# First loads on two queues, gate values behind them, own places for the last batch's second part, and a reordered last group, in an attention and two-layer MoE kernel on one core

## The chip, the cores and the metric

The kernel runs on one core of a Trainium2 chip. The metric is the device time of one execution in microseconds (us), here as the median of several runs. Five engines work side by side: TensorE (PE in the profile, PEld for its weight loads), VectorE (DVE), ScalarE (ACT), GpSimd (POOL) and SyncE (SP). DMA transfers are put in a queue by an engine: rows marked SPq are the instructions of SyncE's queue.

## The reference

The reference is attention with a gated memory, followed by two feed-forward networks over the same 2304 tokens, all in float32:

```
local = softmax(causal(q @ k^T / 8)) @ v                # B=4, H=8, S=576, D=64
qp    = elu(q) + 1
mem   = (qp @ M_prev) / (qp . z_prev + 1e-6)
g     = 1 / (1 + exp(-beta))                            # one gate per head
x     = g * mem + (1 - g) * local                       # 2304 x 512
x     = elu(x @ w_in) @ w_out                           # 512 -> 2048 -> 512
out   = leaky_relu(x @ w2_in, 0.01) @ w2_out            # 512 -> 2048 -> 512
```

The weights come in as float64 and are brought to float32 on the chip.

## The kernel before, in words

**Order of the work.** The function `tile_attn_moe_kernel` traces instructions in an order that is also their priority. A scheduler of the language, which runs when the kernel is built, then puts each engine's instructions into a fixed order by simulated times. On the chip every engine works through its own list in that order, and so does SP with its queue: an instruction that waits holds up all behind it on its engine. `keep_in_program_order(ins)` pins an instruction behind what was traced last on its engine; `issue_after(ins)` puts what a block traces on the engine of `ins` behind `ins` in that engine's list.

**Start.** Before anything else the gate values are made (lines 83 to 87): `beta` is loaded on SP's queue, ScalarE takes the exponential (`ging`), VectorE adds one, takes the reciprocal (`gat`) and makes `omg`. Only `norm` (line 451, `omg`) and `phi_unit` (line 393, `ging`) read them, both later. Attention runs over 4 batches with 4 pairs of heads each. `Pair.load_qk` (lines 265 to 269) loads a pair's keys and then its queries with `load_rows` (line 209), four transfers each, all on SP's queue; `load_rest` loads values, `z_prev` and `M_prev`. TensorE turns keys (`k_unit`, line 294) and queries (`q_unit`, line 312), ScalarE and VectorE copy them out of PSUM, and `score` (line 426) follows.

**Weights.** `load_w` (line 93) fetches a slice f of 128 columns of one network (16 slices) into `wraw` and decodes it. Behind attention that is a chain on one buffer `wm`: ScalarE line 127, VectorE lines 128, 129 and 132, ScalarE cast (`copy`, line 241), GpSimd line 138 twice; then line 127 of the next slice. Slices 0 to 6 of the first network lie in the pool `wpa` and are decoded during attention. Slices 7 to 15 lie in `wpb`, in places w0 to w8, where attention's tiles were before.

**First network, narrow part.** `phase1_units(ti)` (line 663) works on batch ti in two parts of 288 tokens, with slices 0 to 6. `u_load` (line 667) fetches a part: for batches 1 to 3 the attention result lies in two arrays in DRAM (`xq_scr`), so four transfers bring tile `x` and its mirror `y`. `u_x` (line 678) adds `y` to `x` (line 682, four instructions on VectorE), casts to `xh` on ScalarE (line 610) and takes the rest `xl` on GpSimd (line 614). `u_h` (matmuls of line 621, elu of lines 631 to 636 with the cast `gh` at line 243 and `gl` at line 628) and `u_o` (matmuls of line 649) follow. There is one tile `x` and one tile `y` for both parts; the second part's load is traced after slice 1 of the first part, its `u_x` before slice 4 in the last batch, elsewhere before slice 6.

**Last batch.** What is left of the units after attention is the list `side` (line 781). The loop of lines 796 and 797 traces units until `u_x` of the last batch's first part has noted its last cast as `pools["cast", 0]`; the first two decodes of slices 7 and 8 are traced under `issue_after` of that cast (line 800).

**First network, wide part.** Lines 849 to 893 run over five groups of tokens (512 each, the last 256) with slices 7 to 15: line 621 with `xw` and `xv`, elu, line 649 into four PSUM banks. The next group's `h` matmuls use other input tiles and can go before. **Second network.** Lines 899 to 932: per group 16 slices of line 621, `leaky`, and `emit_o3` (matmuls of line 911), one slice after the other with all token blocks (`tb`) of 128 in each. At the end of a group each bank goes out in two halves through a tile `st` with two buffers: VectorE copy (line 931), store on SP's queue (line 932). The last group has two blocks.

Of the kernel before, what the change touches and what calls it, by code (L numbers as in the profile page):

```python
# [8 lines left out]
F32 = mybir.dt.float32  # L9
# [6 lines left out]
P = 128  # L16
# [3 lines left out]
def _f(ap):  # L20
    return ap.bitcast(F32)
# [3 lines left out]
def kernel(  # L25
# [54 lines left out]
    gat = const.tile([P, H], F32, name="gat")  # L80
    ging = const.tile([P, H], F32, name="ging")
    omg = const.tile([P, H], F32, name="omg")
    nc.sync.dma_start(bet, beta.partition_broadcast(P))
    nc.scalar.activation(out=ging, in_=bet, func=AF.Exp, scale=-1.0)
    nc.vector.tensor_scalar(out=ging, in0=ging, scalar1=1.0, scalar2=None, op0=ALU.add)
    nc.vector.reciprocal(gat, ging)
    nc.vector.tensor_scalar(out=omg, in0=gat, scalar1=-1.0, scalar2=1.0, op0=ALU.mult, op1=ALU.add)


    wi_tiles = {}  # L90
    wo_tiles = {}
# [114 lines left out]
    def bank(tag):  # L206
        return psum.tile([P, 512], F32, tag=tag, bufs=BANKS[tag], name=tag)

    def load_rows(dst, src, b, hp, dup):

        hs = slice(2 * hp, 2 * hp + 2)
        for ca, cb, r0 in ((0, 2 if dup else 3, 0), (3, 5, 320)):
            for j in range(2):
                nc.sync.dma_start(
                    dst[:, ca:cb, j * D:(j + 1) * D],
                    src[b, 2 * hp + j, r0:r0 + (cb - ca) * P, :].rearrange("(c p) d -> p c d", p=P),
                )
        for r in range(2 if dup else 0):
            nc.sync.dma_start(
                dst[64 * r:64 * r + 64, 2, :].rearrange("p (j d) -> p j d", j=2),  # L220
                src[b, hs, 256:320, :].rearrange("j p d -> p j d"),
            )
# [29 lines left out]
    class Pair:  # L252
# [12 lines left out]
        def load_qk(self):  # L265
            self.q = at.tile([P, 5, P], F32, tag="qn", bufs=1, name="qn")
            self.k = at.tile([P, 5, P], F32, tag="kn", bufs=1, name="kn")
            load_rows(self.k, k, self.b, self.hp, False)
            load_rows(self.q, q, self.b, self.hp, False)

        def load_rest(self):
            b, hp = self.b, self.hp
# [277 lines left out]
    def attention_units():  # L550

        pairs = [Pair(ti, hp) for ti in range(len(tiles1)) for hp in range(NHP)]
        keys = [(pr, j, g) for pr in pairs for j in range(2) for g in pr.groups]
        items = [Item(*key, n) for n, key in enumerate(keys)]
        first = {}
        for n, it in enumerate(items):
            first.setdefault(id(it.pr), n)
        units = [(0, pairs[0].load_qk, None), (0, pairs[0].load_rest, None)]
        def prep(pi):
            pr = pairs[pi]  # L560
            l = [(PC, lambda g=g: pr.k_unit(g)) for g in pr.kgroups]
            l += [(PC, lambda g=g: pr.q_unit(g)) for g in pr.groups]
            l += [(0, pr.phi_unit)]
            if pi + 1 < len(pairs):
                l.append((0, pairs[pi + 1].load_qk))
            return l

        units += [(c, u, None) for c, u in prep(0)]
        for n in range(len(items) + 2):
            lists = []  # L570
            if n < len(items):
                it = items[n]
                pr = it.pr
                pi = pairs.index(pr)
                head = []
                if first[id(pr)] == n:
                    head.append((0, pr.v_unit))
                    if pi + 1 < len(pairs):
                        head.append((0, pairs[pi + 1].load_rest))
                if n + 1 < len(items) and items[n + 1].pr is not pr:  # L580
                    lists.append(("prep", prep(pi + 1)))
                lists.append(("score", head + it.stages()[0]))
            if 1 <= n <= len(items):
                lists.append(("tr", items[n - 1].stages()[1]))
            if n >= 2:
                it = items[n - 2]
                c = list(it.stages()[2])
                if first[id(it.pr)] == n - 2:
                    c = [(PC, lambda g=g, pr=it.pr: pr.qp_unit(g)) for g in it.pr.groups] + c
                lists.append(("pv", c))  # L590
            w = weave(*lists)
            done = None
            if n >= 2 and (n == len(items) + 1 or items[n - 1].pr.ti != items[n - 2].pr.ti):
                done = items[n - 2].pr.ti
            units += [(c, u, None) for c, u in w[:-1]] + [(w[-1][0], w[-1][1], done)]
        return units
# [4 lines left out]
    def mtile(tag, bufs, dt=F32, shape=None):  # L601
        shape = shape or (NW,)
        pool = pools.get(("own", tag), pools["mlp"])
        return pool.tile([P] + list(shape), dt, tag=tag, bufs=bufs, name=tag)
# [58 lines left out]
    def phase1_units(ti):  # L663

        mine = [(pi, o, w, {}) for pi, (pt, o, w, _) in enumerate(parts) if pt == ti]

        def u_load(pi, o, w, st):
            xt = st["t"] = mtile("x", 1, F32, (NKC, NW))[:, :, 0:w]
            if ti < V32:
                nc.sync.dma_start(xt, xm_scr[ti][:, :, o:o + w])  # L670
                return
            x2 = st["t2"] = mtile("y", 1, F32, (NKC, NW))[:, :, 0:w]
            for j in range(2):
                ps, pz = slice(64 * j, 64 * j + 64), slice(64 - 64 * j, 128 - 64 * j)
                nc.sync.dma_start(xt[ps], xq_scr[ti][j][ps, :, o:o + w])
                nc.sync.dma_start(x2[ps], xq_scr[ti][j][pz, :, o:o + w])

        def u_x(pi, o, w, st):
            xt = st["t"]
            if ti >= V32:  # L680
                for c in range(NKC):
                    add = nc.vector.tensor_tensor(out=xt[:, c], in0=xt[:, c], in1=st["t2"][:, c], op=ALU.add)
                    if c == 0 or ti < len(tiles1) - 1:
                        tc.keep_in_program_order(add)
            st["x"] = split_x(xt, w, pi % 2)
            for n in range(2):
                nc.sync.dma_start(xp_scr[n][pi], _f(st["x"][n]))
            st["g"] = {}

        units = [(0, lambda: u_x(*mine[0]))]  # L690
        for k, (pi, o, w, st) in enumerate(mine):

            def u_h(f, w=w, st=st):
                ph = h_bank()[:, 0:w]
                h_mm(ph, wi_tiles[0, f], *st["x"])
                st["g"][f] = elu(ph, w)

            def u_o(ec, pi=pi, w=w, st=st):
                py = bank("sc" if tail else "pm")[:, 0:w]
                o_mm(py, range(NFA), 0, ec, st["g"], 0, NFA - 1)  # L700
                y = mtile("st", 2)[:, 0:w]
                copy(E_Y, y, py)
                nc.sync.dma_start(y_scr[pi][:, ec], y)

            for f in range(NFA):
                units.append((HC * 12 * w / 2.4, lambda f=f, u=u_h: u(f)))
                if k + 1 < len(mine) and f == 1:
                    units.append((0, lambda k=k: u_load(*mine[k + 1])))
                if k + 1 < len(mine) and f == NFA - (4 if ti == len(tiles1) - 1 else 2):
                    units.append((0, lambda k=k: u_x(*mine[k + 1])))  # L710
            for ec in range(NKC):
                units.append((3 * NFA * w / 2.4, lambda ec=ec, u=u_o: u(ec)))
        return lambda: u_load(*mine[0]), units
# [65 lines left out]
            with tc.high_priority(offset=FILL_OFF):  # L779
                u2()  # L780
    side = [(c, u) for _, c, u in fill]
    del pools["cast", 0]
    attn.close()
    attending = False
    edge = ctx.enter_context(tc.tile_pool(name="edge2", bufs=1, side="right"))
# [7 lines left out]

    wun = [(1, lambda f=f: load_w(0, wpb, w1i, w1o, f, f - NFA)) for f in range(NFA, NF)]
    tail = True
    while ("cast", 0) not in pools:
        side.pop(0)[1]()
    cast = pools["cast", 0]

    def decode_after(unit):  # L800
        with tc.issue_after(cast):
# [98 lines left out]
    for gi, (t0, w) in enumerate(wide):  # L900
        pos = {}
        gs = {}

        def emit_o3(f):
            wo = wo_tiles[1, f]
            gh, gl = gs.pop(f)
            for tb in range(w // P):
                if f == 0:
                    pos[tb] = bank(("sc", "sc", "sc", "po")[tb])
                for n_mm, (wj, gg) in enumerate(((0, gh), (1, gh), (0, gl))):  # L910
                    nc.tensor.matmul(  # L911
                        pos[tb], gg[:, tb * P:(tb + 1) * P], wo[:, wj, :],
                        start=f == 0 and n_mm == 0, stop=f == NF - 1 and n_mm == 2,
                    )

        for f in range(NF):
            ph = h_bank()[:, 0:w]
            h_mm(ph, wi_tiles[1, f], *cur)
            gs[f] = leaky(ph, w)
            if f > 1:  # L920
                emit_o3(f - 2)
        emit_o3(NF - 2)
        if gi + 1 < len(wide):
            cur = load3(*wide[gi + 1])
        emit_o3(NF - 1)
        for tb in range(w // P):
            r0 = t0 + tb * P
# [35 lines left out]
```

## Time and profile before

| | us |
|---|---|
| median of 3 runs | 1073.85 |
| lowest, highest run | 1071.97, 1074.58 |
| the profiled execution's own time | 1071.83 |
| its span, first to last instruction | 1070.0 |
| PE busy | 1041.1 (97%) |
| DVE, POOL, ACT busy | 598.1, 533.2, 483.2 |

Times in rows are microseconds from the span's start. A busy share is an average over stages with different limits, so each part of the change is read in its own stage: the first 30 us, the stretch from 385 to 500 us, and the last 10 us. "Idle before" in a row is the time its engine stood still before the instruction, with what ended it.

### The profile page before, as it was taken

The numbers are of one execution on the slowest core, as the hardware profiler recorded it, in microseconds if no ns is written. First come the engines' busy times: TensorE is split into PE (matmuls) and PEld (weight loads), VectorE is DVE, ScalarE is ACT, GpSimd is POOL, SyncE is SP. The second block draws the span as 40 slices with busy tenths as digits, with TensorE's granted clock in tenths as the row PEclk, the third lists the DMA queues.
The fourth block names the chain that finished last, engine by engine and source line by source line (L and its number), as shares of the span: only waits on it lengthen the run. The fifth ranks groups of instructions, "written<-read, shape, count | busy, mean of one in ns | idle before, by whom it ended". The sixth has DMA issues, their size and how long they took to land.

```text
span 1070.0 us, 17330 instructions
## 1 busy us (share of the span) xinstructions
PE 1041.1 (97%) x5904; PEld 910.1 (85%) x5904; DVE 598.1 (56%) x1382; ACT 483.2 (45%) x1169; POOL 533.2 (50%) x674
## 2 busy tenths in 40 slices
PE   7998899999999999999999999999999999999997
PEld 4786799989998998988888889888888888888896
DVE  6889987788888738666662325654322222231232
ACT  5999887787878734454442224332211211111011
POOL 7675775677668536564542225855422422222221
PEclk9999999999999999999999999999999999999999
DMA  7654543564455248666571304430200200000010
GB/s 183 195 148 113 165 133 101 134 166 141 119 135 153 90 144 265 231 217 195 198 235 41 118 1 138 158 119 1 79 1 1 66 14 1 10 30 1 1 40 20
DMA packets 150408, 115.05 MB, mean 108 GB/s; under 512 B 80048, under 2 KB 142000, under 8 KB 150320
## 3 DMA queue, kind: packets, MB, share of 16 engines
q1 hardware_dynamic: 150320, 113.94, 35.9%
q8 instruction: 47, 0.77, 0.3%
q14 instruction: 41, 0.34, 0.1%
HBM read 78.52 MB, written 31.85 MB: 103 GB/s over the span
## 4 chain that ended last, share of the span: by engine, by line
PE 85%; DVE 6%; DMA 4%; ACT 2%; issue 1%; SPq 1%; POOL 1%; DVEq 0%; ACTq 0%
PE pm L621 19%; PE tp L621 15%; PE sc L911 14%; PE sc L649 9%; PE pm L649 5%; PE po L911 4%; PE po L524 4%; PE tp L457 4%; PE po L649 3%; PE pm L524 2%; PE sc L428 1%; PE sc L429 1%; PE sc L426 1%; DMA y<-xq 1%; DVE pt L431 1%
## 5 line engine op out<-in xcount | busy, mean ns | idle before, releaser
L628 POOL TENSOR_TENSOR gl<-e,gh 128x512 fp32r<-128x512 f32 (+2 forms) x181 | 202.1, 1120 | 379.2 <-DVE gh L243 254.1
L621 PE MATMUL tp<-xw,w 128*128 128x512 f32 (+1 forms) x504 | 144.1, 367 | 0.0
L621 PE MATMUL pm<-xw,w 128*128 128x512 f32 (+1 forms) x496 | 141.9, 368 | 0.0
L911 PE MATMUL sc<-w,gh 128*128 128x512 f32 x448 | 135.9, 390 | 0.0
L451 POOL TENSOR_SCALAR pt<-pt,rs,omg 128x128 f32<-128x128 f32 (+4 forms) x160 | 103.7, 657 | 21.8 <-DVE rs L446 17.9
L649 PE MATMUL sc<-gh,w 128*128 128x512 f32 (+2 forms) x438 | 105.1, 340 | 2.6 <-DVE gh L243 2.6
L621 PEld LDWEIGHTS tp<-xw,w 128*128 128x128 f32 x504 | 91.8, 188 | 16.2
L621 PEld LDWEIGHTS pm<-xw,w 128*128 128x128 f32 x496 | 90.5, 188 | 16.3
L436 ACT ACTIVATE pt<-pt,mx 128x128 f32<-128x128 f32 (+4 forms) x160 | 93.3, 584 | 23.2 <-DVE mx L431 21.6
L911 PEld LDWEIGHTS sc<-w,gh 128*128 128x128 f32 x448 | 83.1, 188 | 16.5
L621 PE MATMUL tp<-xv,w 128*128 128x512 f32 (+1 forms) x252 | 92.5, 367 | 0.0
L621 PE MATMUL pm<-xv,w 128*128 128x512 f32 (+1 forms) x248 | 91.4, 369 | 0.0
L640 ACT ACTIVATE e<-pm 128x512 f32<-128x512 f32 (+1 forms) x40 | 22.2, 555 | 143.4 <-PE pm L621 140.4
L457 PE MATMUL tp<-ident,pt 128*128 128x128 f32 x480 | 81.8, 275 | 3.1 <-DVE al L250 1.5
L641 DVE TENSOR_TENSOR e<-tp,e 128x512 f32<-128x512 f32 (+1 forms) x40 | 25.5, 637 | 106.1 <-ACT e L640 106.0
L649 PEld LDWEIGHTS sc<-gh,w 128*128 128x128 f32 x438 | 74.8, 188 | 11.5 <-DVE gh L243 2.8
L911 PE MATMUL sc<-w,gl 128*128 128x512 f32 x224 | 84.3, 389 | 0.0
L138 POOL TENSOR_TENSOR w<-wm,w 128x512 fp32r<-128x512 f32 x50 | 65.6, 1334 | 34.3 <-ACT w L241 30.1
L243 DVE CAST gh<-e 128x512 fp32r<-128x512 f32 (+2 forms) x146 | 75.4, 520 | 12.9 <-PE po L911 2.2
L641 DVE TENSOR_TENSOR e<-pm,e 128x512 f32<-128x512 f32 (+1 forms) x40 | 25.5, 636 | 101.8 <-ACT e L640 101.8
L621 PE MATMUL pm<-xh,w 128*128 128x288 f32 x368 | 80.3, 304 | 1.9 <-ACT xh L610 1.6
L640 ACT ACTIVATE e<-tp 128x512 f32<-128x512 f32 (+1 forms) x40 | 22.1, 553 | 117.2 <-PE tp L621 113.8
(157 smaller groups left out, 2449.2 us busy)
## 6 DMA issues: line engine op xcount, KB each, us to landing
wraw<-in_moe_w_in_dram SPq DMA_DIRECT2D x32, 512.0 KB, 4.1
wraw<-in_moe_w_out_dram SPq DMA_DIRECT2D x32, 512.0 KB, 5.0
xh<-xh SPq DMA_DIRECT2D x8, 576.0 KB, 3.4
xl<-xl SPq DMA_DIRECT2D x8, 576.0 KB, 3.8
ys<-st SPq DMA_DIRECT2D x32, 144.0 KB, 2.8
x<-x1s SPq DMA_DIRECT2D x9, 512.0 KB, 3.6
out_dram<-st SPq DMA_DIRECT2D x36, 128.0 KB, 1.7
vn<-in_v_dram SPq DMA_DIRECT2D x64, 64.0 KB, 2.4
```

The source lines that it names most:

```text
L138: nc.gpsimd.tensor_tensor(out=w[:, 1, a], in0=t[:, a], in1=_f(w)[:, 0, a], op=ALU.subtract)
L243: (nc.vector if eng == "V" else nc.gpsimd).tensor_copy(dst, src)
L436: nc.scalar.activation(out=pt[0:m, 0:nk], in_=pt[0:m, 0:nk], func=AF.Exp, scale=-1.0, bias=mx[0:m, last:last + 1], accum_out=self.pd["ss"] ...
L451: nc.gpsimd.tensor_scalar(out=pt, in0=pt, scalar1=rs[0:m, i:i + 1], scalar2=omg[0:m, h:h + 1], op0=ALU.mult, op1=ALU.mult,)
L457: nc.tensor.transpose(dst, self.p[c][:, k0:k0 + kn], ident)
L524: nc.tensor.matmul(po[:, a:b], w, x, start=i == 0, stop=i == len(mms) - 1)
L621: nc.tensor.matmul(ph, wi[:, wj, kc, :], xx[:, kc, :], start=n_mm == 0, stop=n_mm == 11)
L628: nc.gpsimd.tensor_tensor(out=gl, in0=g, in1=_f(gh), op=ALU.subtract)
L640: nc.scalar.mul(t, ph, 0.01)
L641: nc.vector.tensor_tensor(out=t, in0=ph, in1=t, op=ALU.max)
L649: nc.tensor.matmul(py, wo[:, wj, ec * P:(ec + 1) * P], gg, start=opens and f == first and n_mm == 0, stop=closes and f == last and n_mm == 2,)
L911: nc.tensor.matmul(pos[tb], gg[:, tb * P:(tb + 1) * P], wo[:, wj, :], start=f == 0 and n_mm == 0, stop=f == NF - 1 and n_mm == 2,)
```

## The change

It has four parts. The first pair's queries are loaded on ScalarE's queue (other pairs' stay on SP's), and the gate values are traced after the first pair's keys and queries. In the last batch the second part's `x` and `y` get places of their own, w8 and w7 of `wpb`, its load is traced first of all units of that batch, and all its adds are pinned. The first two decodes are queued behind the second part's casts (`"cast", 1`) in place of the first part's. In the last group of the second network the last two slices are multiplied block by block; each block is then copied by ScalarE and VectorE, half each, into one tile `ends` and stored in one transfer, block 0 on SP's queue, block 1 on ScalarE's.

```diff
+    def gates():
+        nc.sync.dma_start(bet, beta.partition_broadcast(P))
...
-    def load_rows(dst, src, b, hp, dup):
+    def load_rows(dst, src, b, hp, dup, eng=nc.sync):
...
-                nc.sync.dma_start(
+                eng.dma_start(
...
-            load_rows(self.q, q, self.b, self.hp, False)
+            load_rows(self.q, q, self.b, self.hp, False, nc.sync if self.ti or self.hp else nc.scalar)
...
-        units = [(0, pairs[0].load_qk, None), (0, pairs[0].load_rest, None)]
+        units = [(0, pairs[0].load_qk, None), (0, gates, None), (0, pairs[0].load_rest, None)]
...
+        closing = ti == len(tiles1) - 1
+
+        def rows(tag, pi, w):
+            if not (closing and pi == mine[1][0]):
+                return mtile(tag, 1, F32, (NKC, NW))[:, :, 0:w]
+            slot = NF - NFA - 1 - "xy".index(tag)
+            t = _f(wpb.tile([P, 2, 2, DM], F32R, tag=f"w{slot}", name=f"w{slot}")).rearrange("p a b n -> p (a b n)")
+            return t[:, 0:NKC * NW].rearrange("p (c n) -> p c n", c=NKC)[:, :, 0:w]
...
-                    if c == 0 or ti < len(tiles1) - 1:
+                    if c == 0 or not closing or pi == mine[1][0]:
...
-        units = [(0, lambda: u_x(*mine[0]))]
+        units = [(0, lambda: u_load(*mine[1]))] if closing else []
+        units.append((0, lambda: u_x(*mine[0])))
...
-                if k + 1 < len(mine) and f == 1:
+                if k + 1 < len(mine) and f == 1 and not closing:
...
-    while ("cast", 0) not in pools:
+    while ("cast", 1) not in pools:
         side.pop(0)[1]()
-    cast = pools["cast", 0]
+    cast = pools["cast", 1]
...
+        if gi + 1 == len(wide):
+            ends = mtile("y", 1, F32, (w // P, DM))
+            for tb in range(w // P):
+                for f in (NF - 2, NF - 1):
+                    out_mm(f, tb, *gs[f])
+                for hf, eng in enumerate("AV"):
+                    cs = slice(hf * DM // 2, (hf + 1) * DM // 2)
+                    copy(eng, ends[:, tb, cs], pos[tb][:, cs])
+                (nc.scalar if tb % 2 else nc.sync).dma_start(out[t0 + tb * P:t0 + (tb + 1) * P, :], ends[:, tb])
+            break
```

## Rows read from the trace of the kernel before

**Rows 1.** Profile page: busy time of each engine, share of the span, instructions.
```profile
PE 1041.1 (97%) x5904; PEld 910.1 (85%) x5904; DVE 598.1 (56%) x1382; ACT 483.2 (45%) x1169; POOL 533.2 (50%) x674
```
**Rows 2.** Windows by stage: busy time of PE, PEld, DVE, ACT, POOL, PE clock, DMA.
```profile
0.00:30.00 30.00, 21.53 (x81) 13.52 (x82) 20.69 (x69) 18.71 (x50) 20.95 (x52) 0.94 0.67 172
...
400.00:430.00 30.00, 27.27 (x190) 26.55 (x188) 23.00 (x28) 15.72 (x32) 21.09 (x19) 0.94 0.85 277
430.00:1060.00 630.00, 629.99 (x3028) 532.85 (x3029) 245.93 (x379) 157.78 (x267) 244.11 (x211) 1.00 0.24 79
1060.00:1070.00 10.00, 4.21 (x19) 3.14 (x18) 2.33 (x6) 0.39 (x1) 0.74 (x1) 0.84 0.15 52
```
**Rows 3.** Timeline, first 8 us: start, us, engine, line, operation, idle before.
```profile
0.72 1.28 ACT L84 ACT_TABLE_LOAD   x1 [0.72 <-PEq L947]
...
0.72 0.40 SPq L83 DMA_DIRECT2D bet<-in_beta_dram  x1
...
1.17 2.00 SPq L214 DMA_DIRECT2D kn<-in_k_dram  x4
...
3.22 2.04 SPq L214 DMA_DIRECT2D qn<-in_q_dram  x4
3.30 0.21 ACT L84 ACTIVATE ging<-bet 128x8 f32<-128x8 f32 x1 [1.30 <-DMA bet<-in_beta_dram]
...
4.16 1.31 PE L294 MATMUL sc<-ident,kn 128*128 128x128 f32 x5 [4.16 <-DMA kn<-in_k_dram]
...
4.86 0.37 ACT L296 COPY kk<-sc 128x256 f32<-128x256 f32 x1 [1.35 <-PE sc L294]
...
6.43 1.41 PE L312 MATMUL sc<-ident,qn 128*128 128x128 f32 x5 [0.95 <-DMA qn<-in_q_dram]
...
7.63 5.32 PE L426 MATMUL sc<-kk,q 128*128 128x128 f32 x12
```
**Rows 4.** Chain that ended last, 390 to 425 us: the second part's way.
```profile
405.72 8.02 DMA x<-xq
...
414.97 4.26 DVE x L682 x4
```
**Rows 5.** Timeline of TensorE, 414 to 428 us.
```profile
420.10 1.06 PE L649 MATMUL sc<-gh,w 128*128 128x288 f32 x6 [2.57 <-DVE gh L243]
```
**Rows 6.** Windows, columns as in rows 2: the stretch with the lower clock.
```profile
420.00:425.00 5.00, 4.90 (x25) 4.90 (x26) 4.83 (x6) 0.74 (x1) 5.00 (x5) 0.66 0.31 121
```
**Rows 7.** Timelines of ScalarE and VectorE: starts of the decode chain, elu of slice 3.
```profile
400.19 1.15 ACT L127 ACTIVATE wm<-wraw 128x1024 f32<-128x1024 f32 x1 [0.76 <-DMA wraw<-in_moe_w_out_dram]
...
408.95 1.15 ACT L127 ACTIVATE wm<-wraw 128x1024 f32<-128x1024 f32 x1 [1.38 <-POOL w L138]
...
488.88 1.13 ACT L127 ACTIVATE wm<-wraw 128x1024 f32<-128x1024 f32 x1 [3.03 <-POOL w L138]
...
396.79 2.18 DVE L682 TENSOR_TENSOR x<-x,y 128x288 f32<-128x288 f32 x4 [6.80 <-DMA y<-xq]
...
409.00 0.44 DVE L635 SCALAR_TENSOR_TENSOR e<-e,pm 128x288 f32<-128x288 f32 x1
```
**Rows 8.** Timeline of TensorE around slice 15 of the first wide group.
```profile
488.86 0.39 PE L621 MATMUL tp<-xw,w 128*128 128x512 f32 x1
...
495.21 0.62 PE L621 MATMUL pm<-xw,w 128*128 128x512 f32 x2
```
**Rows 9.** Groups by line, 440 to 500 us: busy, mean ns, idle before.
```profile
L628 POOL TENSOR_TENSOR gl<-e,gh 128x512 fp32r<-128x512 f32 (+1 forms) x12 | 15.4, 1300 | 9.3 <-DVE gh L243 8.9 <-PE tp L621 0.5
```
**Rows 10.** Timeline at the end of the span.
```profile
1064.02 0.76 DVE L931 COPY st<-sc 128x256 f32<-128x256 f32 x2 [2.58 <-PE sc L911]
1064.47 3.06 SPq L932 DMA_DIRECT2D out_dram<-st  x4
1066.27 0.90 DVE L931 COPY st<-sc 128x256 f32<-128x256 f32 x2 [1.49 <-DMA out_dram<-st]
```
**Rows 11.** Chain that ended last, its store at the end.
```profile
1064.47 1.68 DMA out_dram<-st
```

More of the change, by code (lines that the diff above doesn't have):

```diff
@@ L82 @@
     omg = const.tile([P, H], F32, name="omg")
[L83 to L87, printed above, removed]
+    def gates():
+        nc.sync.dma_start(bet, beta.partition_broadcast(P))
+        nc.scalar.activation(out=ging, in_=bet, func=AF.Exp, scale=-1.0)
+        nc.vector.tensor_scalar(out=ging, in0=ging, scalar1=1.0, scalar2=None, op0=ALU.add)
+        nc.vector.reciprocal(gat, ging)
+        nc.vector.tensor_scalar(out=omg, in0=gat, scalar1=-1.0, scalar2=1.0, op0=ALU.mult, op1=ALU.add)
     wi_tiles = {}
@@ L665, in phase1_units @@
         mine = [(pi, o, w, {}) for pi, (pt, o, w, _) in enumerate(parts) if pt == ti]
+        closing = ti == len(tiles1) - 1
[5 more added lines that the diff above has]
+            return t[:, 0:NKC * NW].rearrange("p (c n) -> p c n", c=NKC)[:, :, 0:w]
         def u_load(pi, o, w, st):
-            xt = st["t"] = mtile("x", 1, F32, (NKC, NW))[:, :, 0:w]
+            xt = st["t"] = rows("x", pi, w)
             if ti < V32:
@@ L671, in u_load @@
                 return
-            x2 = st["t2"] = mtile("y", 1, F32, (NKC, NW))[:, :, 0:w]
+            x2 = st["t2"] = rows("y", pi, w)
             for j in range(2):
@@ L706, in phase1_units @@
                 units.append((HC * 12 * w / 2.4, lambda f=f, u=u_h: u(f)))
-                if k + 1 < len(mine) and f == 1:
+                if k + 1 < len(mine) and f == 1 and not closing:
                     units.append((0, lambda k=k: u_load(*mine[k + 1])))
-                if k + 1 < len(mine) and f == NFA - (4 if ti == len(tiles1) - 1 else 2):
+                if k + 1 < len(mine) and f == NFA - (4 if closing else 2):
                     units.append((0, lambda k=k: u_x(*mine[k + 1])))
@@ L781 @@
     side = [(c, u) for _, c, u in fill]
-    del pools["cast", 0]
+    del pools["cast", 1]
     attn.close()
@@ L902, with out_mm @@
         gs = {}
+        def out_mm(f, tb, gh, gl):
+            wo = wo_tiles[1, f]
+            if f == 0:
+                pos[tb] = bank(("sc", "sc", "sc", "po")[tb])
+            for n_mm, (wj, gg) in enumerate(((0, gh), (1, gh), (0, gl))):
+                nc.tensor.matmul(
+                    pos[tb], gg[:, tb * P:(tb + 1) * P], wo[:, wj, :],
+                    start=f == 0 and n_mm == 0, stop=f == NF - 1 and n_mm == 2,
+                )
         def emit_o3(f):
-            wo = wo_tiles[1, f]
-            gh, gl = gs.pop(f)
+            g = gs.pop(f)
             for tb in range(w // P):
[L908 to L914, printed above, removed]
+                out_mm(f, tb, *g)
         for f in range(NF):
@@ L921 @@
                 emit_o3(f - 2)
+        if gi + 1 == len(wide):
[8 more added lines that the diff above has]
+            break
         emit_o3(NF - 2)
-        if gi + 1 < len(wide):
-            cur = load3(*wide[gi + 1])
+        cur = load3(*wide[gi + 1])
         emit_o3(NF - 1)
```

## Prediction

> **What bounds the kernel now.** I read the busy times first: TensorE is busy 1041.1 of 1070.0 us [rows 1]. So a change pays where TensorE stands still or runs at a lower clock, some 29 us of idle time in all. The windows by stage say where that lies [rows 2]: 8.5 us in the first 30, 2.7 between 400 and 430, nothing between 430 and 1060, 5.8 in the last ten. The rest, some 12 us, is spread over the attention stretch, which the change touches only by shifting it. The parts of the change fall on the first three places, so each can pay; and as TensorE is full from 430 to 1060, time won before 430 reaches the end unless a new wait eats it there.
>
> In the first 8 us the timeline shows SP issuing one transfer after the other: beta 0.40 us, four of keys 2.00, four of queries 2.04 [rows 3]. TensorE starts on keys at 4.16, on queries at 6.43, on scores at 7.63. Values and weights come behind all of these in SP's queue.
>
> Around 415 the chain that ended last follows the last batch's second part: its last load is issued at 405.72, lands 8.02 us later, four adds take 4.26 us, [rows 4], and a `gh` cast of the first part stands behind them on VectorE. TensorE waits 2.57 us for that cast [rows 5], and of the slice right behind, 420 to 425, only 0.66 of the clock was granted [rows 6], part of it at 1.2 instead of 2.4 GHz. At the end, copies and stores take turns: two copies, a store, and two more copies that wait for it [rows 10].
>
> **Start: queries on ScalarE's queue, beta behind.** Off SP's queue ahead of the values and weights come four issues, 2.04 us; beta's 0.40 moves from before the keys to behind them. Keys start 0.45 us earlier. The four issues come to ScalarE's list. Its queue shows no transfer before, so their price there is bounded by SP's: 0.51 each. From 0.72 on, 2.04 plus the table load's 1.28 [rows 3] end at 4.04, before the first copy of keys (4.86, then 4.41): hidden. At twice the price they end at 6.1 and the copy comes 1.2 later than now; so the bounds reach a loss. `ging` waits for beta, which landed 2.6 us after its issue began (0.72 to 3.30); issued at 2.7 it is there at 5.3. If the exponential sits before the copies of keys in ScalarE's list, these wait to 5.5, some 0.6 us late against now, and scores gain only from the queries. The three small VectorE instructions then run in the gap before the query copies. Who waits for the gate values is the first `norm`, several us later.
>
> Queries issued at 0.72 are there when TensorE has turned the keys, so the first scores come at about 6.2 in place of 7.63: 1.4 us. SP's later issues, the values and first weights, come 2.04 us earlier. I take **1.5 us**, between 1.4 and 2.0 and nearer to what TensorE's first scores show, with bounds from 1.2 lost to 2.0 gained. The Trainium skill speaks against more ("DMA: Bandwidth & Descriptors", Issuing engines are not separate DMA queues): transfers from several engines share the same 16 DMA engines and interleave, so only issue time is saved. By that rule the keys' last pieces would come later by a part of the queries' transfer, the start would gain next to nothing, and the sum below would be about 4.5 in place of 6; no row before shows two queues at work.
>
> **Middle: own places for the second part.** Before, the second load waits until the first part has left tiles `x` and `y`. Now it is issued right behind the first part's, near 393 to 395, before the weight transfers. It adds four issues of about 0.55 us there, which were there later anyway. Its data should land near 400. The four adds are pinned behind slice 3's elu of the first part, whose add-and-max ran at 409.00 [rows 7]; without a decode beside it perhaps at 407.5. So the adds take 2.2 us (the first part's four, alone) to 4.3 (the second's, beside GpSimd) between 408 and 412, not 415 to 419. The `gh` cast that TensorE waited for comes in time. Gone are the 2.57 us of idle time and what the lower clock cost, (1 - 0.66) x 5 = 1.7 us: **4.3 us**.
>
> **Middle: decodes behind the second casts.** This is the added wait. Line 127 of slice 7, now at 400.19 [rows 7], is put behind casts that follow adds at 408 to 412: it starts near 411, some 10.7 us late, and with it the decodes of nine slices, which hang on one buffer `wm`. Now they take 400.19 to 488.88, 9.9 us each. TensorE uses slice 15 at 488.86 [rows 8], as soon as it is decoded: no slack. Part of the delay is won back, for the chain no longer shares VectorE, ScalarE and GpSimd with the first part's elu, adds and casts; at 9.5 us each slice 15 is there at 411 + 85.5 = 496.5, 7.6 late. TensorE comes 4.3 us earlier, so it lacks 11.9 us of work. What can it do meanwhile? Matmuls there start 0.23 us apart (one takes 0.39, two take 0.62 [rows 8]). So slice 15's last eleven end by 491.4; from there to 495.21 it worked off other slices, 3.8 us, and at 495.21 began the next group's first slice, 12 matmuls, 2.8 us; three such slices fit the four PSUM banks of `h`, 8.3 us. That is 12.1 us, just enough, but then nothing covers the elu of slice 15 (an estimate of 3.5 us: 1.3 for `gl` [rows 9] and four shorter steps on ScalarE and VectorE). I take a new wait of **2.2 us**, between none and 3.5 plus some cover missed.
>
> **End.** The matmuls are the same 12, in another order: block 0 is done 6 x 0.23 = 1.4 us before block 1, and its copies and store lie beside block 1. After the last matmul (1064.0) come two half copies side by side, 0.45 us, one store and the close. From the end of the last copy (1066.27 + 0.90 = 1067.17) to the span's end it took 2.83 us; so 1064.0 + 0.45 + 2.83 = 1067.3, a gain of 2.7. The store is twice as large and goes by ScalarE's queue, which no row shows: between nothing and, at the full 1.68 us that a store took [rows 11], as much again for the second half. I take 0.3 and a gain of **2.4 us**, bounds 1.0 and 2.7.
>
> **Sum.** -1.5 - 4.3 + 2.2 - 2.4 = -6.0 us against the profiled execution's 1071.83 (span 1070.0 and 1.8 around it): 1065.8. The median of the runs stands 2.0 us above that execution, so the forecast is 1073.85 - 6.0 = **1067.8**.
>
> **Rivals.** *The decodes keep up.* If the chain runs at the 8.76 us of its first slice (400.19 to 408.95 [rows 7]), slice 15 is there at 489.8; TensorE then lacks 5.2 us of work, less than its cover, and nothing new waits: 1073.85 - 8.2 = 1065.6. For it: the chain will share its engines with less. Against it: 9.9 us on average now.
>
> *The load does not come earlier.* Places w8 and w7 lie where attention's tiles were, and SP's list may hold the load behind stores or weight transfers; or order changes elsewhere take back the middle's gain. Then start and end alone remain: 1073.85 - 3.9 = 1069.9; with the start lost as well, 1071.4. For it: a transfer took 8.02 us to land there [rows 4]. Against it: the first part's adds begin at 396.79 [rows 7], and they need the same stores.
>
> *The decodes become the bound (slower).* The list of TensorE is fixed when the kernel is built. If it does not hold the next group's matmuls before slice 15's, a chain that is 10.7 us late in full is waited for in full: the 4.3 us are swallowed and 10.7 added. 1073.85 - 3.9 + 10.7 = 1080.6. It decides for slower once slice 15 comes more than 3.9 us later than 488.9 without cover. For it: no slack now. Against it: TensorE's list filled the time to 495.21 with matmuls of other slices [rows 8].
>
> **How the numbers follow.** About 0.3%, 3.2 us, is what a measurement of this kernel can tell from no change. The forecast has 0.48, the decodes keeping up 0.22, the load not earlier 0.20, the decodes as the bound 0.10. Under 1070.6 lie nearly all of the first two and a part of the third: faster 0.73. Over 1077.1 lies most of the last: slower 0.08. The rest, 0.19, is the same. The range runs from 1064.0 (all parts at their best, 2.0 + 4.3 + 2.7 = 9.0, give 1064.8, and the runs spread by 1) to 1072.5 (start and middle both lost, a poor end); it leaves out the slower case and little else. The likeliest case alone would span 1065 to 1070.
>
> **What would show it.** Right: scores near 6.2 us; four transfers from ScalarE's queue; no wait of line 649 for `gh` near 417, a clock of 1.00 there; line 127 of slice 7 near 411; a span that ends 3.3 to 3.6 us after the last matmul. Wrong: TensorE idle between 470 and 500 for decoded weights (line 241 or 138) by more than 5 us; slice 7's decode still near 400; the lower clock again near 420; keys turned later than 4.2 us.

## The result, and the profile after

The change makes the kernel slower by 1%: 1083.05 us in the median of six runs (1082.07 to 1085.79) against 1073.13 of six runs of the kernel before, a ratio of 1.0099 with an interval of 1.0085 to 1.0112. The forecast was 1067.8, so it missed in sign. The profiled execution took 1085.29, 2.2 above the median; its span is 1083.5, that of before 1070.0. The difference of the spans, 13.5, is what the traces have to account for; the medians differ by 9.9, as this execution lies 2.2 above its median and that of before 1.3 below. One execution each of e6, e13 and e15 below took 1.7 to 3.7 ms and is left out of their times and ratios. Line numbers have moved: 127 is 128 after the change, 426 is 427, 621 is 622, 682 is 692 and 911 is 920.

TensorE has the same 5904 matmuls, and its busy time is a little longer than in [rows 1], so the rest of the loss is idle time:

```profile
PE 1047.2 (97%) x5904; PEld 914.6 (84%) x5904; DVE 594.0 (55%) x1380; ACT 483.3 (45%) x1171; POOL 534.3 (49%) x674
```

The windows by stage, columns as in [rows 2], of the kernel after:

```profile
0.00:30.00 30.00, 22.49 (x101) 15.38 (x102) 22.03 (x72) 20.93 (x57) 21.65 (x52) 1.00 0.71 178
30.00:100.00 70.00, 65.22 (x368) 51.16 (x366) 58.65 (x171) 61.69 (x170) 46.26 (x81) 1.00 0.55 149
100.00:200.00 100.00, 93.65 (x681) 87.99 (x682) 83.17 (x254) 80.27 (x232) 68.09 (x109) 0.97 0.45 123
200.00:300.00 100.00, 95.95 (x715) 93.03 (x714) 83.66 (x250) 75.37 (x218) 69.19 (x107) 0.97 0.52 137
300.00:400.00 100.00, 96.07 (x717) 93.39 (x717) 77.53 (x218) 66.92 (x189) 60.06 (x92) 0.97 0.42 116
400.00:430.00 30.00, 29.85 (x224) 29.55 (x223) 14.96 (x27) 11.92 (x29) 14.56 (x17) 1.00 0.87 269
430.00:1060.00 630.00, 624.65 (x2995) 527.18 (x2994) 248.94 (x380) 163.25 (x271) 249.48 (x213) 1.00 0.26 84
```

And the attention stretch of the kernel before, which stands in no group above:

```profile
30.00:100.00 70.00, 67.92 (x385) 54.08 (x383) 62.40 (x176) 64.61 (x182) 45.59 (x81) 1.00 0.56 153
100.00:200.00 100.00, 95.14 (x711) 89.36 (x712) 85.42 (x257) 80.89 (x230) 71.31 (x114) 1.00 0.50 136
200.00:300.00 100.00, 97.34 (x749) 94.48 (x748) 86.72 (x263) 81.02 (x235) 71.59 (x114) 1.00 0.56 144
300.00:400.00 100.00, 97.66 (x751) 96.07 (x750) 71.57 (x206) 64.12 (x179) 57.83 (x85) 1.00 0.44 124
```

Read them stage by stage. The two stages that the change aimed at improved: in the first 30 us TensorE is busy 22.49 in place of 21.53, and from 400 to 430 it is busy 29.85 of 30 in place of 27.27. The loss is where the change edits nothing: in each of the four attention windows TensorE is busy 1.4 to 2.7 us less, and part of three of them runs at the lower of its two clock levels. After that there is a new gap: from 430 to 1060 it is 5.3 us short, where it had been full.

One number per stage says the same more sharply. For a time in the trace of before I counted the matmul columns that TensorE had worked off, and looked when another kernel had worked off as many: the difference is its **lag** (us, positive is late). All lags below are worked out like this from the matmul records of the two profiled executions.

```
time in before      30    100    200    310    400    440    500   1060
after             -3.9   -0.1   +3.3   +7.9  +13.3   +8.3  +15.1  +15.1
```

So the account of the 13.5 us by stages is: attention +13.3, 400 to 440 us -5.0 (where the own places act), 440 to 500 us +6.8 (where the decodes are late), end -1.6 (13.5 less 15.1).

The start itself went nearly as forecast. Timeline of the kernel after, first 7 us:

```profile
0.72 2.12 ACTq L215 DMA_DIRECT2D qn<-in_q_dram  x4
0.72 2.02 SPq L215 DMA_DIRECT2D kn<-in_k_dram  x4
2.87 1.28 ACT L297 ACT_TABLE_LOAD   x1 [2.87 <-issue]
4.35 0.88 PE L295 MATMUL sc<-ident,kn 128*128 128x128 f32 x3 [4.35 <-POOL pt L197]
5.02 0.93 PE L313 MATMUL sc<-ident,qn 128*128 128x128 f32 x3
6.60 0.20 ACT L86 ACTIVATE ging<-bet 128x8 f32<-128x8 f32 x1
6.66 1.27 PE L427 MATMUL sc<-kk,q 128*128 128x128 f32 x3
```

Scores begin at 6.66 in place of 7.63 [rows 3]. At 30 us TensorE is even 3.9 us ahead, and at 100 us all of it is gone.

### The profile page after: what moved, and what is told of

Its sections match the earlier page's. It is cut to its first block, busy times and chain, and to the rows that moved or that the text cites. A ratio compares the mean times of both kernels' runs of the same rounds, so it can differ in the third digit from the quotient of the medians.

```text
span 1083.5 us, 17385 instructions
## 1 busy us (share of the span) xinstructions
PE 1047.2 (97%) x5904; PEld 914.6 (84%) x5904; DVE 594.0 (55%) x1380; ACT 483.3 (45%) x1171; POOL 534.3 (49%) x674
## 4 chain that ended last, share of the span: by engine, by line
PE 77%; DVE 8%; DMA 4%; ACT 4%; issue 3%; POOL 3%; SPq 1%; DVEq 0%; POOLq 0%; ACTq 0%
PE pm L622 18%; PE sc L920 14%; PE tp L622 14%; PE sc L650 7%; PE pm L650 5%; PE po L920 4%; PE po L525 3%; PE tp L458 3%; PE po L650 2%; PE pm L525 2%; PE sc L429 1%; PE sc L430 1%; POOL w L139 1%; PE sc L427 1%; DMA x<-xm 1%
## 5 line engine op out<-in xcount | busy, mean ns | idle before, releaser
L437 ACT ACTIVATE pt<-pt,mx 128x576 f32<-128x576 f32 (+4 forms) x160 | 93.5, 587 | 26.0 <-DVE mx L432 22.5
L244 DVE CAST gh<-e 128x512 fp32r<-128x512 f32 (+2 forms) x146 | 71.9, 496 | 13.0 <-PE po L920 3.1
```

The source lines that it names most:

```text
L244: (nc.vector if eng == "V" else nc.gpsimd).tensor_copy(dst, src)
L437: nc.scalar.activation(out=pt[0:m, 0:nk], in_=pt[0:m, 0:nk], func=AF.Exp, scale=-1.0, bias=mx[0:m, last:last + 1], accum_out=self.pd["ss"] ...
```

## The experiments

After the first look two theories stood. **Theory A**: the edits of the start change the simulated times by which the scheduler orders each engine's list, the whole attention stretch is laid out in another order, and that order is worse. **The rivals, B and C**: one of the two edits costs the time by what it does (B, gate values that come late; C, queries on ScalarE's queue). In the texts of e1 and e2, B is an older rival: that the edits for the last batch make the loss. The first four kernels each hold one part of the change.

**e1, the start alone.**

```diff
...
-            load_rows(self.q, q, self.b, self.hp, False)
+            load_rows(self.q, q, self.b, self.hp, False, nc.sync if self.ti or self.hp else nc.scalar)
...
-        units = [(0, pairs[0].load_qk, None), (0, pairs[0].load_rest, None)]
+        units = [(0, pairs[0].load_qk, None), (0, gates, None), (0, pairs[0].load_rest, None)]
```

> Only the start part: the first pair's queries on ScalarE's queue, gate values behind keys and queries; all else as before. Theory A (these edits lead the scheduler to another order of the whole attention stretch, with more waits of TensorE and spells at the lower clock): first scores near 6.7 us as in the changed kernel, yet the last attention store 10 to 15 us later than before, and the time 9 to 15 us above before. Theory B (the loss in the attention stretch comes from the edits for the last batch): 1 to 2 us faster than before.

Measured: 1080.5 us, ratio 1.0073 (1.0054 to 1.0092). The start by itself loses 8.1 us, a little less than theory A's 9 to 15, and the older B falls. Its lead of 3.9 us is gone by 60 us; its lag is 0.0 at 100 us, 2.5 at 200, 6.1 at 310 and 10.9 at 400, and 7.8 from 440 on: 3.1 us come back there with nothing edited, in the place where before waits for `gh` [rows 5] and e1, which is this late, does not.

**e2, the middle alone**: own places, and the first two decodes behind the second casts.

```diff
...
-            xt = st["t"] = mtile("x", 1, F32, (NKC, NW))[:, :, 0:w]
+            xt = st["t"] = rows("x", pi, w)
...
-        units = [(0, lambda: u_x(*mine[0]))]
+        units = [(0, lambda: u_load(*mine[1]))] if closing else []
+        units.append((0, lambda: u_x(*mine[0])))
...
-    del pools["cast", 0]
+    del pools["cast", 1]
...
```

> Only the middle part: own places, pinned adds, load first, decodes behind the second part's casts. Theory A: attention as before; about 5 us won by 445 us and about 7 lost by 500 us, as TensorE waits for slices decoded late, so 0 to 4 us above before. Theory B: 10 us or more above before, lost between 100 and 400 us. A third reading, that the decodes were late in the changed kernel only because all came late: 4 to 5 us faster than before.

Measured: 1070.87, ratio 0.9985 (0.9975 to 0.9995). The lag is -0.6 at 400, -5.6 at 440 and -1.5 from 500 on: 5.0 us won, 4.1 given back, which lies between theory A and the third reading. The timelines of ScalarE and VectorE show both halves; the adds of the second part come 8 us earlier than at 414.97 [rows 4], and slice 7's decode right behind the last second cast:

```profile
406.92 3.42 DVE L691 TENSOR_TENSOR w<-w,w 128x288 f32<-128x288 f32 x4
410.37 0.43 ACT L610 CAST xh<-w 128x288 fp32r<-128x288 f32 x1 [0.56 <-DVE w L691]
410.71 1.15 ACT L127 ACTIVATE wm<-wraw 128x1024 f32<-128x1024 f32 x1
493.79 1.13 ACT L127 ACTIVATE wm<-wraw 128x1024 f32<-128x1024 f32 x1 [2.64 <-POOL w L138]
```

**e3, the last group alone** (`out_mm` block by block, `ends`, stores on two queues, as in the change).

> Only the last group of the second network in the new order. Both theories: the same up to 1060 us, the span's end 1.6 to 2.7 us earlier, the time 1.5 to 2.7 us below before.

Measured: 1071.0, ratio 0.9986 (0.9977 to 0.9995): 1.4 us, a little under the forecast. The lag is +0.2 at 1060, so the gain lies behind the last matmul.

**e4, own places, but the decodes behind the first casts as before.**

```diff
-    del pools["cast", 1]
+    del pools["cast", 0]
...
-    cast = pools["cast", 1]
+    cast = pools["cast", 0]
```

> As the middle part, but the first two decodes stay behind the first part's casts. If the decodes' place is what gives the middle's gain back: no wait for gh near 417, no lower clock near 422, line 127 of slice 7 within 3 us of its time in before (400.19), and 3 to 5 us below before. If the places themselves hold up the decodes or the places' gain is swallowed by slice 15 anyway: within 1.5 us of before.

Measured: 1077.34, ratio 1.0043 (1.0028 to 1.0058); a miss. Timelines of ScalarE and VectorE, and TensorE's waits from 400 to 560:

```profile
408.56 1.13 ACT L127 ACTIVATE wm<-wraw 128x1024 f32<-128x1024 f32 x1 [3.67 <-DMA wraw<-in_moe_w_out_dram]
414.69 4.33 DVE L691 TENSOR_TENSOR w<-w,w 128x288 f32<-128x288 f32 x4
PE sc L649 <- DVE gh L243: 2.6, 1, 2.6
```

The second part's data is early, but its adds are as late as before, and TensorE waits 2.6 us as in [rows 5]. The load was one of two things that kept the adds late. The other is VectorE's list, in which the decode stands ahead of them, and that decode now waits for weights queued behind the new loads. What makes e4 slower than before comes later: its lag is 0.6 at 457 us and 4.6 at 461, where TensorE waits 2.6 us for an elu (line 635).

**e6, only the queries on ScalarE's queue; e7, only the gate values moved.** Each has one of the two edits of e1.

> The kernel before with the first pair's queries alone on ScalarE's queue; the gate values stay at the start of SP's queue. Theory A (the loss is made by the order of the attention stretch, which is laid out anew after any edit of the start; no single edit has a price of its own): the first scores start 0.5 to 1.0 us earlier than before, and by 400 us TensorE is behind by a number of its own, unlike e1_start's 10.9, anywhere from 0 to 15 us, with the growth at the changes of batch near 100, 220 and 330 us and nothing before 100; span 1070 to 1085 us. Theory B (moved gate values are what costs, and queries on ScalarE's queue are free): lag at 400 us is -1 to 0, span about 1070. Theory C (the queries on ScalarE's queue hold up that engine): lag there from the first 30 us on, near e1_start's.

> The kernel before with the gate values alone moved behind the first pair's keys and queries; the queries stay on SP's queue. Theory A (order laid out anew): the first scores start about 0.5 to 1.5 us earlier than before's 7.6, no lag up to 100 us, then a lag at 400 us of a size of its own, 0 to 15 us, with low-clock spells at other places than before; span 1070 to 1085 us. Theory B (gate values that come later hold up the first normalisation and all behind it): a lag that is there already between 10 and 60 us, and the same 8 to 11 us at 400 us as in e1_start. Theory C (queries on the second queue are the cause): lag at 400 us about 0 and span about 1070.

**e12, keys and queries swapped.** Nothing is added and no queue is touched; the first pair's queries are fetched ahead of its keys.

```diff
-            load_rows(self.k, k, self.b, self.hp, False)
-            load_rows(self.q, q, self.b, self.hp, False)
+            qk = [(self.k, k), (self.q, q)]
+            for dst, src in qk if self.ti or self.hp else qk[::-1]:
+                load_rows(dst, src, self.b, self.hp, False)
```

> The kernel before with the first pair's queries fetched ahead of its keys, on the same queue; no queue, wait or instruction is added, the gate values stay where they were. Theory A (order): the attention stretch is laid out anew all the same; by 400 us TensorE is off by a number of its own (0 to 15 us, most of it from the changes of batch), though the start itself moves by less than 0.5 us; span 1070 to 1085. Theories B and C (one of the two edits of the start costs the time by itself): neither is in this kernel, so it stays within 2 us of the kernel before at 400 us and in its span.

**e8, the change without its start** (e2 and e3 together).

> The change without its start: middle places with the decodes behind the second casts, and the new end. The middle alone measured 1.6 us under the kernel before and the end alone 1.4. All theories: the two are 580 us apart and add, TensorE is at -0.6 to 0 at 400 us, -1.5 at 1060 us, and the time is 3 us under the kernel before, about 1069.5 us (1068.5 to 1070.5). If instead the attention stretch were laid out anew here too, it would be above 1072.

Measured: e6 1075.35 (ratio 1.0033, 1.0016 to 1.0051), e7 1084.8 (1.0118, 1.0103 to 1.0133), e12 1075.5 (1.0036, 1.0026 to 1.0045), e8 1069.71 (0.9978, 0.9968 to 0.9987). In e6 the expected early scores did not come: they begin at 8.55, 0.9 later than before, for ScalarE issued the last two queries only at 3.54, with the table load and the wait for beta between. For the rest theory A holds and B and C fall. Moving the gate values alone costs 12.9 us, more than both edits together (8.1), and the queries alone 3.5: a price that belonged to an edit would add up. A swap that neither B nor C can charge costs 3.6. And e8, whose lists on TensorE, VectorE, ScalarE and GpSimd are in the trace those of before to 400 us (by line, tile and shape), has a lag of only 0.8 there.

**e16, beta's load issued from ScalarE's queue.** In the traces the two lists of TensorE are the same, by line, tile and shape, for 1362 matmuls, to some 226 us, and differ from there on (the text below says 1244 and 209).

```diff
-    nc.sync.dma_start(bet, beta.partition_broadcast(P))
+    nc.scalar.dma_start(bet, beta.partition_broadcast(P))
```

> The kernel before with the one load of beta issued from ScalarE's queue in place of SP's, at the same place; TensorE's order is that of before for its first 1244 matmuls, to about 209 us, and another from there to the end of the attention. Theory A (the order of the attention makes the loss): even with before within 1 us up to 209 us, then off by a number of its own, somewhere between -2 and 8 us by 400 us, taken at the changes of batch near 216 and 322 us. Theory B or C (an edit of the start costs by what it does at the start): even with before all through, or off already by 60 us.

Measured: 1073.9, ratio 1.0028 (1.0016 to 1.0040). The lags of all these kernels:

```
time in before      30    100    200    310    345    400
e1 start          -3.9    0.0   +2.5   +6.1   +9.3  +10.9
e6 queries        -2.8   +1.9   +5.0   +6.0   +6.7   +7.4
e7 gate values    -2.5   +0.7   +4.5   +9.0  +13.8  +14.3
e12 swap          -2.2   -1.1   +1.4   -0.1   +3.8   +4.4
e16 beta's queue  -0.2   -0.2   +0.4   +0.3   +3.8   +4.0
e8 no start       +0.4   -0.2   +0.4   +0.4   +1.3   +0.8
e3 end            -0.3   -0.2   -0.1   -0.1   -0.2   -0.1
```

e16 is the cleanest of them. It moves one transfer in the first microsecond, stays even with before for 320 us, and loses 3.5 us between 310 and 345, long after anything that the edit does itself. (What happens there is read below, with the clock.)

**e13, weights earlier; e15, weights earlier and decodes behind the first casts.** They ask whether the decodes' loss in e8 can be had back. In e13 the transfers of slices 7 and 8 are traced ahead of the casts; e15 also goes back to `"cast", 0`.

```diff
...
+    for f in (NFA, NFA + 1):
+        early[f] = fetch_w(w1i, w1o, f)
     while ("cast", 1) not in pools:
```

> e8_mid_end with the transfers of weight slices 7 and 8 traced ahead of the casts, so that they are queued right behind the second part's loads (in e8 they went at 397.4 to 403.8, between stores). The late decodes cost e2 some 4 us after 443 us. Theory P (ScalarE's order sets them: the decode is listed behind the last of the second part's casts, which in e8 ended at 412.1, where line 127 began): nothing changes, line 127 of slice 7 begins at 412, the time is within 0.5 us of e8's 1069.7. Theory Q (the weights' transfer sets them): line 127 begins some 3 us earlier and 2 to 3 us of TensorE's waits go, about 1067.

> e13_raw_first with the decodes behind the first casts, as before the change. In e4 such decodes failed because the weights had been queued behind the second part's loads and line 127 waited for them 3.67 us to 408.56, the adds behind it till 414.69. Theory P: with the weights queued earlier line 127 of slice 7 begins at 402 to 405, the adds follow at 407 to 411, the wait for the half of g at 420 (2.6 us) goes and no decode is late: TensorE is 4 to 6 us ahead of before from 443 us on, time 1065 to 1067, the best of all. Theory Q (VectorE is the bound in this stretch: whichever of decode and adds goes first, the other is late): within 1 us of e8's 1069.7, or above.

Measured: e13 1071.31, ratio 0.9999 (0.9988 to 1.0010); e15 1072.39, ratio 1.0008 (0.9997 to 1.0019). In e13 line 127 (133 in its text) follows the last second cast, as theory P says, though at 413.56 and not 412, and the 2.2 us that e8 won are gone, which P did not expect. The edit did not queue the weights behind the second part's loads but ahead of them: they are issued from 393.2 and the loads from 396.7 (393.7 in e8), and adds, casts and decode follow 1.4 us later than in e8:

```profile
413.22 0.43 ACT L616 CAST xh<-w 128x288 fp32r<-128x288 f32 x1 [0.55 <-DVE w L697]
413.56 1.14 ACT L133 ACTIVATE wm<-wraw 128x1024 f32<-128x1024 f32 x1
```

In e15 the decode of slice 7 starts at 400.93, with no wait for weights, as early as before. But VectorE takes slice 8's as well (line 133 at 409.67) before the adds, and TensorE's old wait is back:

```profile
415.99 4.34 DVE L697 TENSOR_TENSOR w<-w,w 128x288 f32<-128x288 f32 x4
PE sc L655 <- DVE gh L249: 2.6, 1, 2.6
```

The theory Q of e15 holds for this stretch: adds and decodes compete for VectorE's list, and the one that stands second is late. To have both early would take an order that none of these kernels has.

## Why the prediction was wrong

**The step that failed** is this one: "The rest, some 12 us, is spread over the attention stretch, which the change touches only by shifting it." The edits of the start do not shift that stretch; they make the scheduler lay it out anew. In e1 that costs 10.9 us to 400 us, in the change 13.3. (Up to there the traces of these two show the same order on TensorE, VectorE, ScalarE and GpSimd, so the 2.4 between them are scatter of two executions.) The front of the document says that order comes from simulated times, so an edit of the first load could have been seen to reach every later place in the lists. The prediction gave it half a sentence, under one rival, and no price. None of its rivals is what happened. That the price of the third, 1080.6, comes near the measured time is luck: it rests on the decodes alone.

**How the new order loses the time** I can read but did not test, since any edit that takes work from an engine lays the stretch out anew too. Three readings bear on it. First, VectorE, busy 83 of the first 100 us, has less work done when the first batch ends. From the windows 0 to 100, VectorE's busy time, and TensorE's lag at 110 us:

```
              before   e16    e8  after   e12    e1    e7    e6
VectorE busy   83.09 82.94 82.57  80.68 80.52 80.24 79.68 78.12
lag at 110         0  -0.1  -0.3   +4.0  +2.7  +3.9  +5.5  +6.9
```

Kernels that have before's order there are short by at most 0.5 us and not late; the others are short by 2.4 to 5.0 us and late by 2.7 to 6.9. Second, the wait table of VectorE from 8 to 103 us (us in total, times, longest) says for what it stood still, first before, then e1. It is the decodes of weight slices beside the attention, whose first and fifth steps ScalarE does:

```profile
DVE po L114 <- ACT po L113: 3.5, 5, 1.6
DVE w L122 <- ACT w L241: 2.5, 4, 0.8
```
```profile
DVE po L115 <- ACT po L114: 4.7, 5, 3.0
DVE w L123 <- ACT w L242: 4.6, 7, 1.7
```

That is 6.0 us before and 9.3 in e1. Where a batch changes (near 105, 220 and 325 us) the lags of e1 and of the change rise; most of the first rise is made up again by 130 us (e1 from 3.9 to 0.3), most of the later ones are not.

Third, the lower of TensorE's two clock levels, 1.2 GHz. In e16 the whole late rise falls into one stretch at that level: the lag is 0.5 where it begins, at 324 us, and 4.2 where it ends, at 331. Windows of before, then of e16:

```profile
322.00:337.00 15.00, 13.46 (x100) 12.60 (x101) 13.84 (x44) 12.70 (x39) 13.52 (x20) 1.00 0.87 226
```
```profile
322.00:337.00 15.00, 12.50 (x75) 11.54 (x76) 13.45 (x38) 9.48 (x27) 9.78 (x16) 0.77 0.70 199
```

The stretches at 1.2 GHz near 105 and 330 us hold rises of 1.9 to 3.4 in e1, e12 and the change too; in e8, with the order of before, none holds more than 1.2. Each run's span and mean granted clock are on record, and (1 - clock) times the span is an estimate of what the lower clock can cost: in the mean of the runs 6.0 us before, 5.5 in e8, 7.8 in e16, 8.1 in the change, 8.6 to 8.9 in e1, e12 and e6, 10.6 in e7. The 1.8 more could be most of the 2.6 that e16 loses; the 2.1 more are a small part of the change's 9.9. Whether the new order brings the lower clock about is not shown: from 320 to 325 us TensorE is busy 2.75 us in before and in e16, and only in e16 did the clock fall. Which single place in the lists matters stays open as well.

**Start.** Forecast 1.5 us, measured 1.0 at the first scores (6.66). ScalarE's issues were hidden, as argued: 2.12 us, then the table load. TensorE turned the first keys at 4.35 (4.60 in e1), not at the 3.7 that a start 0.45 earlier would have given; later than 4.2 was one of the prediction's own signs of being wrong. And the gain was worth nothing: in e1 and in the change the lead is gone by 100 us, and the prediction let time won at 6 us reach the end without following it through the attention.

**Middle.** Forecast 4.3, measured 5.0 in e2. (After the change it is 5.0 too, but 3.1 of these come in e1 without any edit here.) The load was issued where forecast (393 to 395; e2 392 to 396), the adds came at 406.92 for 408 and took 3.42, inside 2.2 to 4.3, although the first part's adds, the lower bound, did not run alone: GpSimd's line 614 runs beside them from 397.79. In e2 TensorE is busy all of 400 to 430. What the text had wrong is to whom the gain belongs: e4 and e15 show that the places bring nothing while decodes stand ahead of the adds. It counted the decodes' move as a cost alone; it is a condition of the gain. The move without the places was not run; as the last load lands at 413.74 in [rows 4] and the adds begin at 414.97, it could bring some 1.2 us at most, an estimate.

**Decodes.** The start of the chain was forecast well (411; e2 410.71) and its pace a little too slow (9.5 us a slice; e2 9.2), and yet the new wait was mis-sized: 2.2 forecast, 4.1 measured in e2 and 6.8 after (1.6 of these are in e1 too, whose decodes were not moved). The forecast put all of it at slice 15 and let TensorE's other work cover the rest. TensorE's lag in e2 steps up in three places before that instead, by 1.9 us at 457 to 461, 0.6 by 477 and 1.5 by 485. The third is a wait for a decoded weight (line 241). The first is a wait for an elu (line 635) that frees a PSUM bank; ScalarE's step for it (line 633) comes only at 453.70, behind the cast of a decode (452.75). After the change the waits near 500 are

```profile
497.38 0.50 PE L650 MATMUL sc<-gh,w 128*128 128x512 f32 x1 [2.18 <-DVE gh L244]
507.46 0.96 PE L622 MATMUL tp<-xw,w 128*128 128x512 f32 x3 [1.62 <-ACT w L242]
```

with line 128 of slice 7 at 425.27, 25 us later than in [rows 7], while TensorE is 13.3 late at 400 us and 8.7 at 425.

**End.** Forecast 2.4, measured 1.6 in the change and 1.4 in e3. Timeline of the kernel after, last microseconds:

```profile
1077.80 1.07 PE L920 MATMUL sc<-w,gh 128*128 128x512 f32 x4
1078.71 0.61 PE L920 MATMUL sc<-w,gl 128*128 128x512 f32 x2
1079.54 0.76 DVE L244 COPY y<-sc 128x256 f32<-128x256 f32 x2 [2.98 <-ACT y L242]
1079.99 0.33 SPq L944 DMA_DIRECT2D out_dram<-y  x1
1080.33 0.37 ACTq L944 DMA_DIRECT2D out_dram<-y  x1
```

TensorE's list ends with `gl` matmuls in a pair, as before the change, and VectorE's two half copies run back to back only after that: block 0's copies do not lie beside block 1's matmuls. From the last matmul (1079.32) to the end of the span (1083.5) it takes 4.2 us, not 3.3 to 3.6.

**The sum.** Start +13.3 where -1.5 was forecast (to 400 us), middle -5.0 for -4.3, decodes +6.8 for +2.2, end -1.6 for -2.4. The parts do not add up to the change: measured alone, start, middle and end give 8.1 - 1.6 - 1.4 = 5.1 us, the change 9.9. Beside the new order the middle does not pay: against e1 the change wins 1.8 us from 400 to 440 and loses 5.1 behind 440, where e2 wins 5.0 and loses 4.1. With the start left out (e8), the forecast's other terms give -4.5 and the runs -2.2 (1069.71 against 1071.87). e8 is the best version found, ahead of both kernels.

## What to carry to other kernels

Where a scheduler orders the lists from simulated times, an edit at the start is an edit of everything behind it: five kernels that differ from before only in the work of the first few microseconds (e1, e6, e7, e12, e16) lay between 0.3% and 1.2% above it, and their prices did not add. Nor did the price of a part that is worth something beside the old order (the middle) carry over to the new one. Compare the engines' orders before believing a local sum, try such an edit by itself, and price the risk as a case of its own. A gain from an earlier load also needs its consumer to stand early in its engine's list: the places paid only together with the move of the decodes.

## What the runs showed of the hardware that was not expected

**Two queues slow each other.** From issue to landing a transfer of the first pair's keys took 3.1 us (median of four) in e1 and after the change, with the queries beside it, and 2.3 before and 2.4 in e7, alone; one of the queries took 3.2 and 3.3 beside the keys, and 2.4 and 2.2 alone. With the queries beside them, the keys' turning began at 4.60 us in e1 and waited for the keys; in e7, where the keys go first and alone on SP's queue from the same 0.72 us, it began at 3.75 and waited for a memset:

```profile
4.60 0.87 PE L295 MATMUL sc<-ident,kn 128*128 128x128 f32 x3 [4.60 <-DMA kn<-in_k_dram]
```
```profile
3.75 0.88 PE L295 MATMUL sc<-ident,kn 128*128 128x128 f32 x3 [3.75 <-POOL ms L195]
```

So in e1 the keys were used 0.85 us later. In e6, with beta ahead of the keys as in [rows 3], the turning began at 5.07 in place of 4.16. The Trainium skill has a rule for this ("DMA: Bandwidth & Descriptors", Issuing engines are not separate DMA queues): transfers from several engines run on the same 16 DMA engines and interleave, so that a second issuing engine saves issue time only. The prediction weighed that rule and chose against it; the trace agrees with the rule on the keys, while the first scores of e1 still came 0.7 us earlier (6.91), by the queries.

**Equal clocks, unequal losses.** In e8, TensorE has a granted clock of 0.66 from 102 to 107 us, so part of that stretch is at 1.2 instead of 2.4 GHz, after five microseconds in which it was busy 3.68; before has 1.00 there:

```profile
97.00:102.00 5.00, 3.68 (x25) 2.54 (x23) 4.37 (x14) 4.88 (x16) 4.41 (x7) 1.00 0.31 72
102.00:107.00 5.00, 4.43 (x24) 4.21 (x25) 4.75 (x14) 4.45 (x11) 3.13 (x6) 0.66 0.76 197
```

The lag is -0.2 at 100 us and 0.0 at 105: TensorE is busy 4.43 of these five microseconds where it is busy 3.76 in before, with about as many matmuls (24 and 25), so the slower matmuls took the place of idle time. In the windows from 100 to 400 us the mean clock of e8 is 0.97, 0.98 and 0.98, that of e16 0.97, 1.00 and 0.97, and that of e1 0.97, 0.98 and 0.97; the lags at 400 are 0.8, 4.0 and 10.9. So the mean clock of a stretch does not by itself measure what is lost there: beside idle time it cost little (e8), elsewhere up to 3.7 us in one place (e16). The prediction's way of turning (1 - clock) times the stretch into a gain needs a TensorE that has work all the time.
